# A fused attention, Fourier, MLP and rotation kernel: a layernorm's small values put in PSUM, and single columns and a row of the transform handled in another way

## The chip, the cores and the metric

The kernel runs on one core of one Trainium2 chip. The metric is the device time of one execution in microseconds (us), lower is better; the shown time of a kernel is the median of its runs.

## The reference

Three blocks follow each other. Attention on 2 batches, 8 heads, 768 positions of 64 values, where a query sees only the keys of its own hash bucket (the signs of six projections). Then the real part of a two-dimensional Fourier transform is added, and a layernorm feeds a two-layer MLP. Then an angle per element turns the values into two parts, which are mixed over the positions, and a last layer is added.

```
mask = q_bucket[:, :, :, None] == k_bucket[:, :, None, :]
attn = softmax(where(mask, q @ k^T / 8, -1e9)) ; x = attn @ v        # (2, 768, 512)

mixed = real(fft(fft(x, axis=1), axis=2))
u  = x + mixed
un = (u - mean(u)) / sqrt(var(u) + 1e-6)                               # over the 512 columns
x  = u + relu(un @ w_ch1) @ w_ch2                                      # 512 -> 2048 -> 512

theta = x @ w_theta
y = w_tok_r @ (x * cos(theta)) + w_tok_i @ (x * sin(theta))            # over the 768 rows
u = x + y
out = u + relu(u @ w_ch)
```

## The kernel before

**Number format.** Large matrices are split into a high and a low part (16-bit or a rounded 32-bit format) and multiplied in three passes (high by high, high by low, low by high). That is why many names come as pairs: `w1h`, `w1l`; `hh`, `hl`; `wthh`, `wthl`. The high part is made by ScalarE (ACT), the low part by VectorE (DVE) or GpSimd (POOL), which subtracts the high part from the original.

**Stages.** A batch has six row tiles of 128 x 512. Attention goes by tiles of 128 queries of one head, 48 tiles a batch: scores on TensorE (PE, matmuls `pss<-stk`, four of 128x384 a tile), the row maximum on DVE (`nm`), the exponential on ACT (`p`), its masking on POOL (`p<-p,p`, `pt`), a transposing DMA (`pt<-p`), and the product with the values on PE (`pso<-vv,pt`). The transform (`Fft`) folds the rows on DVE as the heads come in (`fold`, `part`), then `rest` multiplies with the cosine and sine tables on PE (first `ps<-h,ct`, then `psm<-dt,fa`, whose last matmuls of a tile read `hlz`) and adds the result to `u` on DVE. `rest` yields after each of its three column groups, each with two of the six row tiles.

**The layernorm** (`ln_scale`, line 706) works on two row tiles at a time: BN_STATS and BN_AGGR give mean and variance `mv`, and then twelve DVE instructions on 128x2 values compute the inverse square root `rs`: `ve` is the variance plus 1e-6, an integer shift (`t<-ve`) and an integer multiply-add (`rs<-t`) give a first guess, and three Newton steps of three instructions refine it (`t<-rs,ve`, `t<-t,rs`, `rs<-t,rs`). All of it is in SBUF. `ln_first` does this for the first two row tiles of batch zero: DVE makes `un`, PE transposes it (`psm<-ident,un`). The other five pairs go through `layernorm`: ACT and DVE make the two halves of `u2`, and a transposing DMA on the SP queue writes them to `unT`.

**The MLP.** `mlp1` multiplies `unT` with `w1` in tiles of two 128-column groups (`psm<-unT,w1h` and `psm<-unT,w1l`, 24 matmuls of 256 columns), `mlp2` multiplies the result with `w2` (matmuls of 512 columns, called `w2` matmuls below; 96 a group).

**What sets the order.** A framework schedules each engine's instructions from priorities: `at(us)` sets the due time of what is written next, and a model of the machine orders the instructions of each engine. So the MLP of batch zero, the attention of batch one and the transform of batch one are interleaved: the scheduler decides how many MLP matmuls stand between two score tiles, and a change of a few instructions can change that order. PSUM has eight banks, taken in rings: while attention runs, three of one bank each (`psm`, taken by `PS1()` in turn for the transform, the layernorm's transposes and the MLP), two double ones for scores (`pss`) and one for the attention output (`pso`); after it, five more single ones (`psf`).

**Lines the change touches.** `Fft.__init__` (544) makes the fold buffer `fa`; `part` makes the difference or sum of mirrored columns, `one` (574) handles the one column that has no mirror partner; `fold` (580) calls them. In `rest` (612) the transform's last step keeps two lone columns per row tile in exchanged places and swaps them through `lone`, and copies row 0 of tile 3 to `row` before a single-row sum is added. Constants come from `_constants`; its table `so` holds the sines of odd frequencies.

Of the kernel before, what the change touches and what calls it, by code (L numbers as in the profile page):

```python
# [33 lines left out]
def f(t):  # L34
    return t.bitcast(F32)
# [35 lines left out]
def fused_kernel(ctx, tc, A, out):  # L71
# [469 lines left out]
    class Fft:  # L541


        def __init__(self, b, side):
            self.b, self.p = b, pool(f"ft{b}", 1, side=side)
            ft = self.p
            self.fa = mk(ft, [128, 4608], F32, "fa")
            self.fm = self.fa[:, 0:3072].rearrange("p (a n) -> p a n", a=6)
            self.y1 = self.fa[:, 3072:4608].rearrange("p (a n) -> p a n", a=6)
# [23 lines left out]

        def one(self, nm, i, a):

            hl = self.hl[nm][:, :, :, i:i + 1]
            V.tensor_copy(out=hl[:, 0], in_=a)
            V.tensor_tensor(out=hl[:, 1], in0=a, in1=f(hl[:, 0]), op=ALU.subtract)

        def fold(self, p):  # L580
# [20 lines left out]
            if p in (1, 2) and 3 - p in self.done:  # L601
                self.part("e", slice(65, 128), ALU.subtract, y1[:, 0:self.ne, 65:128], y1[:, 0:self.ne, 191:128:-1])
                yield
                self.part("o", slice(64, 127), ALU.add, y1[:, 3:6, 65:128], y1[:, 3:6, 191:128:-1])
                self.one("o", 127, y1[:, 3:6, 128:129])
                yield
            if len(self.done) == 4:
                self.part("e", slice(1, 65), ALU.subtract, y1[:, 0:self.ne, 1:65], y1[:, 0:self.ne, 255:191:-1])
                self.one("e", 0, y1[:, 0:self.ne, 0:1])
                self.part("o", slice(0, 64), ALU.add, y1[:, 3:6, 1:65], y1[:, 3:6, 255:191:-1])  # L610

        def rest(self):
# [3 lines left out]
            if self.ne == 4:  # L616
                er = hl["e"][0:1, :, 3]
            else:

                er = hl["o"][0:1, :, 0]  # L620
                er0 = mk(ft, [1, 128], F32, "zraw", bufs=2 - self.b)
                V.tensor_tensor(out=er0[:, 1:128], in0=y1[0:1, 3, 1:128], in1=y1[0:1, 3, 255:128:-1], op=ALU.subtract)
                V.tensor_copy(out=er0[:, 0:1], in_=y1[0:1, 3, 0:1])
                V.tensor_copy(out=er[:, 0], in_=er0)
                V.tensor_tensor(out=er[:, 1], in0=er0, in1=f(er[:, 0]), op=ALU.subtract)
# [8 lines left out]
            for tt in (0, 3):  # L634
                for c in (0, 256):
                    cc = 192 + (c if tt == 0 else 256 - c)
                    pl_copy(u[:, tt:tt + 3, cc:cc + 1], x[:, tt:tt + 3, c:c + 1])
            alt2 = alt.unsqueeze(1).to_broadcast([1, 193, 2])
            acs = mk(ft, [128, 4608], F32R, "fa")
# [35 lines left out]
            for t in range(3):  # L675
# [11 lines left out]
                if t == 0:  # L687
                    row = mk(ft, [1, DM], F32, "hle")
                    V.tensor_copy(out=row, in_=u[0:1, 3])
# [8 lines left out]
                V.tensor_copy(out=mid, in_=u[:, 3 + t, 448:191:-256])  # L698
                V.tensor_copy(out=u[:, 3 + t, 192:449:256], in_=mid)
# [7 lines left out]
    def ln_scale(b, g, p):  # L707
# [3 lines left out]
        v, r, t = (mk(p, [128, n], F32, f"{k}{g[0]}") for k in ("ve", "rs", "t2"))  # L711
        for i in range(n):
# [4 lines left out]
        V.tensor_scalar(out=t.bitcast(I32), in0=v.bitcast(I32), scalar1=1, scalar2=None, op0=ALU.logical_shift_right)  # L717
        V.tensor_scalar(out=r.bitcast(I32), in0=t.bitcast(I32), scalar1=-1.0, scalar2=1597463007.0,
                        op0=ALU.mult, op1=ALU.add)
# [4 lines left out]
        return mv, r, t  # L724

    def ln_first():

        mv, rs, _ = ln_scale(0, (0, 2), so_p)
# [13 lines left out]
    def layernorm(b, m_p, ln_p, res, groups):  # L742
        u = u_t[b]
        unT = res[b] = mk(m_p, [128, 8, S], F16, "unT")
        for g in groups:
            mv, rs, t2 = ln_scale(b, g, ln_p)
# [326 lines left out]
def _constants():  # L1073
# [15 lines left out]
    s2, so, s0 = cs(np.sin, d, k2), cs(np.sin, d + 1, ko), cs(np.sin, d, k0)  # L1089
    dt = np.concatenate([cs(np.cos, d, k) for k in (k2, ko, k0, ku)] + [  # L1090
# [59 lines left out]
```

## Time and profile before

| | |
|---|---|
| median of three runs | 759.32 us (758.41 to 765.56) |
| profiled execution, device time | 759.25 us |
| its span in the trace | 757.5 us |
| PE busy | 672.4 us, 89% |
| DVE busy | 440.9 us, 58% |
| ACT busy | 400.3 us, 53% |
| POOL busy | 370.7 us, 49% |
| chain that ended last | PE 43%, DVE 15%, issue 12%, ACT 11%, POOL 10%, DMA 9% |

How to read it: busy times are those of one profiled execution, which the trace covers from its first to its last instruction (the span); device time has 1.75 us more around it. The chain that ended last is followed back from the last instruction, at each step to what released it, so its shares name the engines that were waited for. In rows of the trace, `out<-in` are the program's buffer names, shapes are partitions x elements, `xcount` folds equal neighbours on one engine, and `[5.67 <-DVE un L62]` is idle time ahead of an instruction with what ended it. PEclk is the clock that TensorE was granted, as a share of 2.4 GHz.

### The profile page before, as it was taken

The page shows a single profiled execution, that of the slowest core. Times are in us where ns is not written, and L with a number is a line of the kernel's source. Part 1 is how long each engine was busy: PE and PEld are TensorE (multiplying, and loading weights), DVE is VectorE, ACT ScalarE, POOL GpSimd, SP SyncE. Part 2 cuts the span into 40 slices and gives each one's busy share as a digit, 9 for nine tenths or more (in the row PEclk, how much of TensorE's full clock was granted, in tenths as well). Part 3 has the DMA queues.
Part 4 walks back from the last instruction along what each step waited for, and adds up shares of the span by engine and source line. Part 5 has one row for each costly group of instructions (what it writes and reads, how often), then busy time and mean ns, then how long its engine had stood idle before and what let it go on. Part 6 is the DMA issues. An engine that isn't in the chain of part 4 may idle for free.

```text
span 757.5 us, 13333 instructions
## 1 busy us (share of the span) xinstructions
PE 672.4 (89%) x5300; PEld 526.5 (70%) x5300; DVE 440.9 (58%) x710; ACT 400.3 (53%) x639; POOL 370.7 (49%) x302
## 2 busy tenths in 40 slices
PE   6979775859397997999989979999999989999997
PEld 2767564647286555786676757587485778998997
DVE  6778879698889855543386782055332266552122
ACT  4787595967588798763322151064325555662010
POOL 4786778697666779776560110033403235841000
PEclk8999997969689998999999989999999999999999
DMA  9685768479687999878650061011003611362202
GB/s 321 150 171 102 167 126 167 94 207 195 184 183 166 228 239 262 158 141 120 114 184 7 5 157 29 1 42 29 1 1 126 201 29 43 110 217 77 84 1 83
DMA packets 151358, 93.19 MB, mean 123 GB/s; under 512 B 126272, under 2 KB 136704, under 8 KB 151296
## 3 DMA queue, kind: packets, MB, share of 16 engines
q1 hardware_dynamic: 149424, 85.87, 48.3%
q0 software_dynamic: 1872, 6.47, 2.4%
q8 instruction: 41, 0.67, 0.4%
q14 instruction: 21, 0.17, 0.1%
HBM read 49.62 MB, written 6.29 MB: 74 GB/s over the span
## 4 chain that ended last, share of the span: by engine, by line
PE 43%; DVE 15%; issue 12%; ACT 11%; POOL 10%; DMA 9%; POOLq 0%; SPq 0%; ACTq 0%; DVEq 0%
PE psm L62 26%; PE psf L62 10%; DMA r<-in_wtok 3%; ACT r L62 3%; DMA pt<-p 2%; POOL p L62 2%; PE pss L64 2%; DVE fa L64 2%; DVE nm L64 2%; POOL w1l L62 2%; ACT stk L64 2%; DVE r L62 2%; PE psm L64 2%; DVE fa L62 1%; DMA r<-in_w 1%
## 5 line engine op out<-in xcount | busy, mean ns | idle before, releaser
L62 PE MATMUL psm<-unT,w1h 128*128 128x256 f16 x768 | 131.9, 276 | 7.9 <-DMA unT<-u 4.5
L62 PE MATMUL psm<-unT,w1l 128*128 128x256 f16 x384 | 105.9, 276 | 0.0
L62 PEld LDWEIGHTS <-w1h 128*128 128x128 f16 (+1 forms) x774 | 75.6, 99 | 24.3 <-issue 11.6
L62 DVE SCALAR_TENSOR_TENSOR r<-r 128x512 uint32<-128x512 uint32 (+1 forms) x64 | 59.0, 923 | 55.3 <-ACT r L62 49.5
L64 PE MATMUL pss<-stk 128*128 128x384 f32 x192 | 51.4, 390 | 26.6 <-ACT p L64 6.7
L62 POOL TENSOR_TENSOR w1l<-r,w1h 128x384 fp32r<-128x384 f32 (+1 forms) x36 | 41.0, 1148 | 58.4 <-ACT w1h L62 58.2
L62 PEld LDWEIGHTS <-hh 128*128 128x128 f16 x384 | 37.2, 99 | 43.1 <-issue 2.7
L62 DVE TENSOR_REDUCE nm<-pss 128x1 f32<-128x768 f32 x48 | 45.1, 950 | 34.9 <-PE pss L62 34.9
L62 ACT ACTIVATE r<-r,chalf 128x512 uint32<-128x512 uint32 (+1 forms) x64 | 46.2, 722 | 33.1 <-DMA r<-in_wtok 17.0
L62 POOL TENSOR_TENSOR p<-p,p 128x768 f16<-128x768 f32 x32 | 55.3, 1731 | 15.9 <-ACT p L62 14.3
L62 DVE SCALAR_TENSOR_TENSOR hl<-psm,hh 128x512 f16<-128x512 f32 x48 | 32.9, 686 | 48.9 <-ACT hh L62 48.8
L62 PE MATMUL psm<-w2l,hh 128*128 128x512 f16 x192 | 61.2, 385 | 0.0
L62 PE MATMUL psm<-w2h,hl 128*128 128x512 f16 x192 | 61.0, 383 | 0.0
L62 PE MATMUL psm<-w2h,hh 128*128 128x512 f16 x192 | 60.5, 382 | 0.0
L62 ACT ACTIVATE hh<-psm 128x512 f16<-128x512 f32 x48 | 28.4, 592 | 57.6 <-PE psm L62 57.5
L62 ACT ACTIVATE p<-pss,nm 128x768 f32<-128x768 f32 x48 | 42.7, 894 | 27.9 <-DVE nm L62 26.4
L62 PE MATMUL pss<-stk 128*128 128x384 f32 x192 | 50.7, 389 | 7.6 <-ACT p L62 6.4
L64 PEld LDWEIGHTS pss<-stk 128*128 128x128 f32 x192 | 34.4, 207 | 31.1 <-ACT p L64 8.2
L64 DVE TENSOR_REDUCE nm<-pss 128x1 f32<-128x768 f32 x48 | 45.5, 950 | 15.7 <-PE pss L64 15.4
L62 PEld LDWEIGHTS pss<-stk 128*128 128x128 f32 x192 | 35.1, 206 | 12.0 <-ACT p L62 8.9
L62 POOL TENSOR_SCALAR nn<-nn 128x512 f32<-128x512 f32 x12 | 7.9, 655 | 71.1 <-ACT nn L62 71.1
L62 PEld LDWEIGHTS <-w1l 128*128 128x128 f16 x384 | 38.0, 99 | 6.5 <-issue 1.8
(297 smaller groups left out, 1682.9 us busy)
## 6 DMA issues: line engine op xcount, KB each, us to landing
r<-in_w SPq DMA_DIRECT2D x32, 512.0 KB, 4.6
r<-in_wtok SPq DMA_DIRECT2D x24, 384.0 KB, 3.8
stk<-stk SPq DMA_DIRECT2D x28, 192.0 KB, 3.3
vr<-in_v SPq DMA_DIRECT2D x8, 390.0 KB, 4.6
tt<-in_qT SPq DMA_DIRECT2D x8, 384.0 KB, 3.6
tt<-in_kT SPq DMA_DIRECT2D x8, 384.0 KB, 4.4
xT<-xs SPq DMA_DIRECT2D x12, 256.0 KB, 2.6
xt<-xT SPq DMA_DIRECT2D x4, 768.0 KB, 5.6
```

The source lines that it names most:

```text
L62: return fn(*a, **k)
L64: self.last = fn(*a, **k)
```

## The change

*Layernorm.* `ln_scale` takes a PSUM tile `few` from `PS1()` and keeps `ve` and `t` in it; `rs` and `mv` stay in SBUF. The shift is gone: one integer multiply-add by -0.5 makes the first guess, so the chain has 11 instructions. `layernorm` makes its own small `t2` in SBUF for the product of mean and deviation.

*Lone columns.* The fold buffer has a column more in each of six parts, set to zero once, so that the column without a partner meets a zero or, where the sine table's column 127 is halved, itself. `one` and its instructions are gone; `part` works on slices one column wider. In the single-row sum two DVE copies are gone and one is made by ACT.

*Row copy and swaps.* Row 0 of tile 3 is copied by POOL, ahead of the transform's multiplications, to a place that is free by then. The swaps of the lone columns, six pairs of 128x2 copies, are made by ACT in place of DVE.

```diff
-            self.fa = mk(ft, [128, 4608], F32, "fa")
+            self.fa = mk(ft, [128, 4614], F32, "fa")
-            self.y1 = self.fa[:, 3072:4608].rearrange("p (a n) -> p a n", a=6)
+            self.y1 = self.fa[:, 3072:4614].rearrange("p (a n) -> p a n", a=6)
+            V.memset(self.y1[:, :, 256:257], 0.0)
...
-        def one(self, nm, i, a):
-
-            hl = self.hl[nm][:, :, :, i:i + 1]
-            V.tensor_copy(out=hl[:, 0], in_=a)
-            V.tensor_tensor(out=hl[:, 1], in0=a, in1=f(hl[:, 0]), op=ALU.subtract)
...
-                self.part("o", slice(64, 127), ALU.add, y1[:, 3:6, 65:128], y1[:, 3:6, 191:128:-1])
-                self.one("o", 127, y1[:, 3:6, 128:129])
+                self.part("o", slice(64, 128), ALU.add, y1[:, 3:6, 65:129], y1[:, 3:6, 191:127:-1])
...
-                self.part("e", slice(1, 65), ALU.subtract, y1[:, 0:self.ne, 1:65], y1[:, 0:self.ne, 255:191:-1])
-                self.one("e", 0, y1[:, 0:self.ne, 0:1])
+                self.part("e", slice(0, 65), ALU.subtract, y1[:, 0:self.ne, 0:65], y1[:, 0:self.ne, 256:191:-1])
...
-                V.tensor_tensor(out=er0[:, 1:128], in0=y1[0:1, 3, 1:128], in1=y1[0:1, 3, 255:128:-1], op=ALU.subtract)
-                V.tensor_copy(out=er0[:, 0:1], in_=y1[0:1, 3, 0:1])
-                V.tensor_copy(out=er[:, 0], in_=er0)
+                V.tensor_tensor(out=er0, in0=y1[0:1, 3, 0:128], in1=y1[0:1, 3, 256:128:-1], op=ALU.subtract)
+                AC.activation(out=er[:, 0], in_=er0, func=AF.Copy)
...
+            row = x[0:1, 5] if self.b else un0[0:1, 1]
+            pl_copy(row, u[0:1, 3])
...
-                if t == 0:
-                    row = mk(ft, [1, DM], F32, "hle")
-                    V.tensor_copy(out=row, in_=u[0:1, 3])
...
-                V.tensor_copy(out=mid, in_=u[:, 3 + t, 448:191:-256])
-                V.tensor_copy(out=u[:, 3 + t, 192:449:256], in_=mid)
+                AC.activation(out=mid, in_=u[:, 3 + t, 448:191:-256], func=AF.Copy)
+                AC.activation(out=u[:, 3 + t, 192:449:256], in_=mid, func=AF.Copy)
...
-        v, r, t = (mk(p, [128, n], F32, f"{k}{g[0]}") for k in ("ve", "rs", "t2"))
+        r = mk(p, [128, n], F32, f"rs{g[0]}")
+        few = PS1()
+        v, t = few[:, 0:n], few[:, 8:8 + n]
...
-        V.tensor_scalar(out=t.bitcast(I32), in0=v.bitcast(I32), scalar1=1, scalar2=None, op0=ALU.logical_shift_right)
-        V.tensor_scalar(out=r.bitcast(I32), in0=t.bitcast(I32), scalar1=-1.0, scalar2=1597463007.0,
-                        op0=ALU.mult, op1=ALU.add)
+        V.tensor_scalar(out=r.bitcast(I32), in0=v.bitcast(I32), scalar1=-0.5, scalar2=1597463007.0, op0=ALU.mult, op1=ALU.add)
...
+            t2 = mk(ln_p, [128, g[1] - g[0]], F32, f"t2{g[0]}")
...
+    so[127] *= 0.5
```

**Where instructions move.** PE has as many instructions as before, and so has the SP queue; DVE has 28 fewer (684 in place of 712), ACT 13 more, POOL 2 more. PE's order is unchanged up to the first transform matmul of batch zero and again from batch one's MLP on; between them it differs. At the 16th, 24th, 32nd and 48th score tile of batch one, the MLP of batch zero has done 73, 200, 266 and 384 of its 576 first-layer matmuls before, and 0, 170, 208 and 384 after; of its 288 `w2` matmuls 0, 50, 96 and 185 before, and 0, 0, 96 and 132 after. The pieces below show the places that matter. First DVE, from the second BN_AGGR of the first layernorm to `un`; numbers behind names are buffer numbers. Before:

```order
L62 BN_AGGR mv_2278<-bs 128x2
L62 TENSOR_SCALAR ve_2279<-mv_2278 128x2
L62 TENSOR_SCALAR t_2281<-ve_2279 128x2
L62 TENSOR_SCALAR rs_2280<-t_2281 128x2
L62 TENSOR_REDUCE nm<-pss 128x1
L62 TENSOR_TENSOR t_2281<-rs_2280,ve_2279 128x2
L62 SCALAR_TENSOR_TENSOR r_2123<-r_2123 128x512
L62 SCALAR_TENSOR_TENSOR t_2281<-t_2281,rs_2280 128x2
```

The same place after the change, up to the first Newton step:

```order
L62 BN_AGGR mv_2274<-bs 128x2
L62 SCALAR_TENSOR_TENSOR r_2106<-r_2106 128x512
L62 TENSOR_TENSOR x<-pso,r 128x6x64
L62 TENSOR_SCALAR psm<-mv_2274 128x2
L62 TENSOR_REDUCE nm<-pss 128x1
L62 TENSOR_SCALAR rs_2275<-psm 128x2
L62 SCALAR_TENSOR_TENSOR r_2113<-r_2113 128x512
L62 TENSOR_TENSOR psm<-rs_2275,psm 128x2
```

A weight conversion (`r`) and a scaling of attention output (`x`) have come in behind BN_AGGR; before `un` there are in all three conversions, two reductions `nm` and one scaling, where there were one conversion and one reduction. Next PE, at the transposes of the first layernorm (`un_110`), which stood apart around one score tile. Before:

```order
L62 MATMUL pso<-vv,pt 128x65
L62 MATMUL psm<-ident,un_110 128x128 x4
L62 MATMUL pss<-stk 128x384 x4
L62 MATMUL psm<-ident,un_110 128x128 x4
L62 MATMUL psm<-dt,fa 128x2x64 x6
```

After:

```order
L62 MATMUL psm<-ident,un_110 128x128 x8
L62 MATMUL psm<-dt,fa 128x2x64 x6
L62 MATMUL psm<-dt,fa 128x2x128 x6
L62 MATMUL psm<-dt,fa 128x2x64 x3
L62 MATMUL psm<-dt,hlz_2236 128x2x64 x3
L62 MATMUL pss<-stk 128x384 x4
```

The eight transposes now follow each other, all behind the twelfth score tile of batch one, where the first four stood behind the eleventh. Last ACT at the end of batch one's transform, where the swaps stand. Before:

```order
L62 ACTIVATE fa<-psf 128x386
L62 ACTIVATE hlz_5279<-psf 128x384
L62 ACTIVATE wthh<-r_5479 128x512
L62 ACTIVATE wthh<-r_5486 128x512
L62 ACTIVATE wthh<-r_5493 128x512
```

After:

```order
L62 ACTIVATE fa<-psf 128x386
L62 ACTIVATE hlz_5268<-psf 128x384
L62 ACTIVATE lone<-u_5107 128x2
L62 ACTIVATE u_5107<-lone 128x2
L62 ACTIVATE lone<-u_5107 128x2
L62 ACTIVATE u_5107<-lone 128x2
L62 ACTIVATE lone<-u_5107 128x2
L62 ACTIVATE u_5107<-lone 128x2
L62 ACTIVATE wthh<-r_5463 128x512
L62 ACTIVATE wthh<-r_5470 128x512
```

The three pairs of swaps stand ahead of the `wthh` conversions, which make the high part of `w_theta`. In batch zero the swaps stand among exponentials (`p<-pss,nm`) and weight conversions (`w1h<-r`), some of which come between the two copies of a pair. On PE, between the last transform matmul of batch one and the first of batch one's MLP that reads batch one's `unT`, there stood 56 `w2` matmuls and one set of transposes; now 82 `w2` matmuls stand ahead of it.

## Rows read from the trace of the kernel before

**Rows 1.** Stages: us; PE, PEld, DVE, ACT, POOL busy (instructions); PEclk, DMA, GB/s.

```profile
197.00:209.20 12.20, 2.91 (x23) 2.15 (x22) 11.82 (x16) 4.52 (x7) 10.40 (x8) 0.50 0.81 212
209.20:427.10 217.90, 203.46 (x1887) 152.16 (x1887) 135.56 (x219) 129.75 (x190) 133.88 (x101) 0.97 0.73 156
427.10:444.30 17.20, 12.72 (x62) 5.93 (x61) 17.17 (x69) 7.96 (x15) 4.70 (x4) 0.95 0.41 107
444.30:449.60 5.30, 5.25 (x26) 3.83 (x27) 3.62 (x7) 1.43 (x4) 0.42 (x1) 0.52 0.77 151
```

**Rows 2.** Timeline of PE: start, length, instruction, [idle before].

```profile
199.40 1.65 PE L62 MATMUL pss<-stk 128*128 128x384 f32 x4 [2.31 <-ACT p L62]
...
209.22 1.11 PE L62 MATMUL psm<-ident,un 128*128 128x128 f32 x4 [5.67 <-DVE un L62]
```

**Rows 3.** Groups of DVE, 197 to 207.2 us: count, busy us, mean ns.

```profile
L62 DVE SCALAR_TENSOR_TENSOR t<-t,rs 128x2 f32<-128x2 f32 x3 | 1.9, 623 | 0.1
L62 DVE TENSOR_SCALAR t<-ve 128x2 int32<-128x2 int32 x1 | 1.6, 1569 | 0.0
L62 DVE TENSOR_TENSOR t<-rs,ve 128x2 f32<-128x2 f32 x3 | 1.5, 507 | 0.1
L62 DVE TENSOR_SCALAR ve<-mv 128x2 f32<-128x2 f32 x1 | 1.4, 1411 | 0.0
L62 DVE TENSOR_SCALAR rs<-t 128x2 int32<-128x2 int32 x1 | 1.1, 1076 | 0.0
L62 DVE SCALAR_TENSOR_TENSOR rs<-t,rs 128x2 f32<-128x2 f32 x3 | 1.1, 358 | 0.1
L62 DVE TENSOR_REDUCE nm<-pss 128x1 f32<-128x768 f32 x1 | 0.9, 945 | 0.0
L62 DVE SCALAR_TENSOR_TENSOR r<-r 128x512 uint32<-128x512 uint32 x1 | 0.7, 678 | 0.0
```

**Rows 4.** Timeline of DVE at the second layernorm's first chains.

```profile
432.94 1.17 DVE L62 SCALAR_TENSOR_TENSOR t<-t,rs 128x2 f32<-128x2 f32 x1
...
434.11 1.27 DVE L62 TENSOR_SCALAR ve<-mv 128x2 f32<-128x2 f32 x1
...
435.37 1.26 DVE L62 TENSOR_TENSOR t<-rs,ve 128x2 f32<-128x2 f32 x1
...
436.62 0.15 DVE L62 TENSOR_TENSOR t<-rs,ve 128x2 f32<-128x2 f32 x1
```

**Rows 5.** Timeline of POOL beside the two chains.

```profile
196.33 3.68 POOL L62 TENSOR_TENSOR p<-p,p 128x768 f16<-128x768 f32 x2
...
432.77 3.83 POOL L62 TENSOR_TENSOR wthl<-r,wthh 128x512 fp32r<-128x512 f32 x3 [37.59 <-ACT wthh L62]
```

**Rows 6.** Timeline of PE ahead of batch one's MLP.

```profile
438.79 0.59 PE L62 MATMUL psm<-w2h,hl 128*128 128x512 f16 x2
439.22 0.60 PE L62 MATMUL psf<-ident,u 128*128 128x128 f32 x4
444.35 0.59 PE L62 MATMUL psm<-unT,w1h 128*128 128x256 f16 x2 [4.53 <-DMA unT<-u]
```

**Rows 7.** Groups of the whole span: DVE twice, ACT, POOL.

```profile
L62 DVE TENSOR_TENSOR hle<-fa,hle 128x4 fp32r<-128x4 f32 x1 | 2.6, 2554 | 0.0
...
L62 DVE TENSOR_SCALAR r<-pso 128x6 f32<-128x6 f32 x8 | 1.2, 155 | 5.0 <-PE pso L62 5.0
...
L62 ACT ACTIVATE hle<-zraw 128x189 fp32r<-128x189 f32 x1 | 0.4, 360 | 3.1 <-DVE hlo L62 3.1
...
L62 POOL TENSOR_SCALAR u<-x 128x384 f32<-128x384 f32 x4 | 4.1, 1028 | 5.9 <-PE pso L62 5.9
```

**Rows 8.** Timeline of ACT ahead of the second layernorm.

```profile
432.01 1.80 ACT L62 ACTIVATE wthh<-r 128x512 fp32r<-128x512 f32 x3 [10.95 <-DVE mv L62]
```

**Rows 9.** Timeline of DVE: the last value of batch zero's third chain.

```profile
239.42 0.14 DVE L62 SCALAR_TENSOR_TENSOR rs<-t,rs 128x2 f32<-128x2 f32 x1
```

**Rows 10.** Timeline of PE: third MLP tile's start, batch zero.

```profile
226.00 0.38 PE L62 MATMUL psm<-unT,w1h 128*128 128x256 f16 x2
```

More of the change, by code (lines that the diff above doesn't have):

```diff
@@ L637, in rest @@
                     pl_copy(u[:, tt:tt + 3, cc:cc + 1], x[:, tt:tt + 3, c:c + 1])
+            row = x[0:1, 5] if self.b else un0[0:1, 1]
+            pl_copy(row, u[0:1, 3])
             alt2 = alt.unsqueeze(1).to_broadcast([1, 193, 2])
-            acs = mk(ft, [128, 4608], F32R, "fa")
+            acs = mk(ft, [128, 4614], F32R, "fa")
             off = [0]
@@ L723, in ln_scale @@
             V.scalar_tensor_tensor(out=r, in0=t, scalar=1.5, in1=r, op0=ALU.add, op1=ALU.mult)
-        return mv, r, t
+        return mv, r
     def ln_first():
-        mv, rs, _ = ln_scale(0, (0, 2), so_p)
+        mv, rs = ln_scale(0, (0, 2), so_p)
         for i in range(2):
@@ L745, in layernorm @@
         for g in groups:
-            mv, rs, t2 = ln_scale(b, g, ln_p)
+            mv, rs = ln_scale(b, g, ln_p)
+            t2 = mk(ln_p, [128, g[1] - g[0]], F32, f"t2{g[0]}")
             gate[b] = V.scalar_tensor_tensor(out=t2, in0=mv[:, :, 0], scalar=-1.0, in1=rs, op0=ALU.mult, op1=ALU.mult)
```

## The prediction, made before the changed kernel ran

> **What bounds the kernel now.** I read the table of stages first [rows 1]: each row gives the busy time of the engines in a stretch. TensorE (PE) fills most of the span: from 209.2 us to 427.1 it is busy 203.5 of 217.9. In two short stretches it stands. From 197.0 to 209.2 it works 2.9 of 12.2 us while VectorE (DVE) works 11.8; from 427.1 to 444.3 it works 12.7 of 17.2 while DVE works all of it. In both, a layernorm's inverse deviation is computed. So the question is what the change does to these two waits, and whether the time stays won.
>
> The first wait is in PE's timeline [rows 2]: the transposes of `un` start at 209.22 after 5.67 us of idling for DVE. What DVE did is in the grouped rows [rows 3]: 12 instructions on 128x2 values, the chain `ve`, `t`, `rs`, take 8.6 us (1.9 + 1.6 + 1.5 + 1.4 + 1.1 + 1.1). One such instruction takes 0.15 us where nothing holds it (the last line of [rows 4]); the long ones run beside GpSimd (POOL) instructions, such as 3.68 us of `p` [rows 5]. The second layernorm shows it more sharply: three chain instructions last 1.17, 1.27 and 1.26 us [rows 4] while POOL's three `wthl` subtractions run, 3.83 us from 432.77 [rows 5]; the next take 0.15 again. So a DVE instruction of this chain can be held until a POOL instruction ends.
>
> The Trainium skill says this in "SBUF — State Buffer", section "Who interferes with whom": a DVE instruction with two SBUF inputs, or in a two-port mode, contends with a GpSimd instruction that reads SBUF, and one with a single SBUF input outside those modes does not. The trace agrees for the held side (1.17 against 0.15 us); no row of before has these instructions with an operand in PSUM.
>
> The second wait is 4.53 us for the transposed `unT` [rows 6]. Behind it PE runs at half clock: 444.3 to 449.6 has a granted clock of 0.52, nearly all at the lower level of 1.2 GHz [rows 1].
>
> **The change, part by part.**
>
> *Chain values in PSUM.* With no hold left, the first chain falls from 8.6 us to 11 instructions of 0.15, that is 1.7: 6.9 us won. With full hold nothing is won. I take the end near no hold: the held rows read only SBUF, often twice, and no new instruction of the chain has two SBUF inputs (`t` and `v` are in PSUM, `r` and `mv` in SBUF). For the price of a PSUM operand the nearest row reads PSUM on 128x6 in 155 ns [rows 7], no more than SBUF; a write of small values to PSUM is in no row, so I bound it by nothing and by another 0.15 us an instruction, 1.7 us a chain, and take nothing. `un` and the weight conversions keep SBUF operands and can still be held.
>
> The Trainium skill has a rule against the change: "Perfetto Trace Analysis", section "Optimizing Scalar/DVE Operations", puts DVE's access overhead at about 60 ns on SBUF and 125 on PSUM. By it 11 instructions would cost 0.7 us more (an estimate from that page), inside the bound above; the row with a PSUM source shows no such difference.
>
> *Order around the first chain.* DVE's order now has two conversions `r`, one reduction `nm` and one scaling `x` more between the second aggregate and `un`. At 0.68 and 0.95 us [rows 3], the scaling taken as a conversion, they take back 3.0 of the 6.9 us, though that work is not owed later. PE's wait of 5.67 us shrinks by 3.9 to 5.67; I take 4.5.
>
> *Order around the second chain.* The three holds lie 3.3 us above 3 x 0.15 [rows 4]. More follows from PE's order: between the last transform matmul and the first that needs `unT` stood 56 `w2` matmuls and one set of transposes; now 82 `w2` matmuls stand there. At two every 0.43 us [rows 6] they are 17.6 us of work. `unT` came 17.2 us after the last transform matmul (427.1 to 444.3), and should now come after some 13.9. Either is under 17.6, so the wait of 4.53 goes even if the chain wins nothing. With it goes the half clock: 5.3 us at 0.52 lose 2.5. Together 7.0.
>
> *What covers it must come from somewhere.* PE's instructions are the same in number. When the second batch's last scores are issued, 132 of the MLP's `w2` matmuls stand ahead of them instead of 185: 53 fewer, 11.5 us at 0.216. That work comes later, so PE has less to fill its earlier gaps with. From 209.2 to 427.1 it idles 14.4 us already [rows 1]. If the softmax of the second batch moves up as far as PE's work is taken out, nothing is lost; if not, 11.5 us are. The engines of the softmax were busy 62% (DVE, 135.6 of 217.9) and 61% (POOL), PE 93%, so PE mostly set the pace: I take 2.5.
>
> *Swaps on ScalarE (ACT).* Six pairs, at most 0.36 us an instruction by the nearest row, of 189 columns [rows 7]. ACT waits there for DVE's add. Behind it queue, in batch zero, an exponential or weight conversion, which the score tiles wait for; in batch one, three `wthh` conversions, which already stood idle 10.95 us for this place [rows 8]. DVE adds other tiles meanwhile; only the last pair before a chain is uncovered, 0.7 us, and in batch one the `w2` work covers that. Uncovered, all would cost 12 x 0.36 = 4.3.
>
> *Lone columns and row copy.* Of the removed DVE instructions one was dear because it was held: 2.55 us for the four-column subtraction [rows 7]. A neighbour with two SBUF inputs inherits such a hold, so I count 0.5 of a possible 2.5, swaps included. POOL's copies of one row cost about what its copies of 384 columns do, 1.03 us [rows 7], off the path: the copy is needed a whole group of matmuls later. The ACT copy in the single-row sum is hidden the same way, the two memsets (nearest row 128x6, 0.155 us [rows 7]) stand where DVE is not waited for, the parts are a column wider, and the halved constant is made on the host: nothing.
>
> *The rest.* PE's order is the same row by row up to the first transform matmul of batch zero at 160.8 us, and from batch one's MLP at 444.3 to the end. A difference must arise between.
>
> The sum: 4.5 + 7.0 + 0.5 - 2.5 = 9.5 us off 759.25, the profiled execution's own time (span 757.5 plus 1.75 around it; the median of the runs is 759.32). That is 749.8.
>
> **The rivals.**
>
> *First gain absorbed.* Behind 209 us PE, DMA, POOL and ACT take turns, so the 4.5 us may be waited for elsewhere, and the small gain too. What is left is 7.0 - 2.5: 754.8. It also holds if the chain stays held in PSUM, so that the change doesn't do what it says, since the cover of the second wait does not depend on it. For it speaks that PE waited 2.31 us for an ACT-made operand in the same stretch [rows 2].
>
> *Filler missed.* The second batch's softmax does not move up, and PE idles the whole 11.5 us: 759.25 - 4.5 - 7.0 + 11.5 = 759.2. Against it speaks PE's 93%.
>
> *Slower: the bank that holds the chain.* The chain's values now keep one of three `psm` banks until `rs` is done. The MLP's tiles of batch zero come behind the second and third chain in that ring. Before, the third chain's last `rs` was written at 239.42, while the third tile's matmuls began at 226.00 [rows 9, 10]. If the chains run no faster and this order stays, PE stands from 226.0 to 239.6, 13.6 us, and runs cold for another 2.5 behind it. With the first and small gains gone: 759.25 - 7.0 + 13.6 + 2.5 = 768.4. It decides from a wait of about 14 us in all. Against it: in the new order the MLP begins four softmax tiles later, after most of these chains.
>
> **How the numbers follow.** Forecast 0.53, absorbed 0.20, filler missed 0.15, bank 0.12. About 1% (7.6 us) is what a measurement of this kernel tells from no change. Faster, under 751.7, is the forecast's share, 0.53; slower, over 766.9, the bank's, less a little, 0.11; the rest 0.36. The range runs from 743 (waits of 5.67 and 7.0 gone, 4 from the small parts' bounds, nothing given back, gives 742.6) to 762 (filler missed with a first gain of only 1.7); that leaves out the bank's case and a tail of the others. The forecast's own range is 743 to 752.
>
> **What would show it.** Chain instructions of about 0.15 us beside busy POOL show the PSUM step right; of 1 us, wrong. No wait for `un` over 1.5 us shows the first gain. PE without a gap before batch one's MLP, and a clock of 1.0 there, shows the second; if that MLP then begins later than some 437 us, the filler was missed. A PE wait for `rs` at batch zero's second or third MLP tile shows the bank. The forecast is wrong if PE's idle time between 209 and 427 grows by over 5 us.

## The result, and the profile after

The changed kernel takes 754.34 us, the median of eight runs (750.65 to 756.07), against 759.96 us before, taken on the same chip. The ratio is 0.9911 with a 95% interval of [0.9883, 0.9939]: 5.6 us less. A second set of six runs gave 754.42 us and 0.9912 [0.9882, 0.9941]. The execution that was profiled first is the fastest of the fourteen, 750.65 us with a span of 748.6; the second profiled one took 753.04 us with a span of 751.2.

The table of stages, cut at the same matmuls in both kernels: from the first transform matmul of batch zero to the transposes of `un`, from there to the last score matmul of batch one, and to the last transform matmul of batch one. What stands between two cuts is not quite the same, since PE's order differs: in the changed kernel one score tile more with its products stands in the first stage, and in the second that tile and 53 `w2` matmuls are missing. Columns as in [rows 1]. Before:

```profile
160.82:209.22 48.40, 33.84 (x229) 26.67 (x229) 43.82 (x57) 32.49 (x52) 35.07 (x25) 0.71 0.75 184
209.22:372.66 163.44, 151.39 (x1472) 110.14 (x1473) 100.76 (x152) 117.76 (x167) 119.49 (x82) 0.95 0.88 181
372.66:427.29 54.63, 52.26 (x418) 42.16 (x416) 34.96 (x67) 11.99 (x23) 14.38 (x19) 1.00 0.29 80
```

After, with two stages more, from the last transform matmul to the first matmul of batch one's MLP, and the 5.3 us behind that:

```profile
160.55:203.26 42.71, 35.14 (x272) 28.03 (x272) 34.06 (x55) 35.11 (x58) 34.75 (x25) 0.78 0.79 186
203.26:362.87 159.61, 139.85 (x1381) 104.73 (x1379) 98.82 (x144) 116.16 (x168) 121.03 (x84) 0.95 0.92 192
362.87:419.38 56.51, 55.32 (x433) 43.02 (x431) 34.30 (x61) 12.10 (x26) 14.66 (x21) 1.00 0.29 77
419.38:436.92 17.54, 17.54 (x82) 7.92 (x81) 15.33 (x63) 9.74 (x19) 5.10 (x4) 1.00 0.51 123
436.92:442.22 5.30, 5.30 (x38) 3.64 (x37) 2.05 (x4) 2.98 (x5) 0.00 (x0) 1.00 1.03 188
```

The last two rows answer to the last two of [rows 1]: PE now works through, at a clock of 1.00 where 0.95 and 0.52 stood. The stage ahead of batch one's MLP is no shorter for it, 17.5 us against 17.1 (427.29 to 444.35): the wait is filled with `w2` matmuls from earlier stages. The first row is 5.7 us shorter. The second is shorter by 3.8 us, but PE is idle in it for 19.8 us (159.61 less 139.85), where it was idle for 12.1.

PE's timeline of the changed kernel, which answers to [rows 2] and [rows 6]:

```profile
203.26 1.09 PE L62 MATMUL psm<-ident,un 128*128 128x128 f32 x4
204.76 1.09 PE L62 MATMUL psm<-ident,un 128*128 128x128 f32 x4 [0.41 <-DVE un L62]
...
224.27 1.65 PE L62 MATMUL pss<-stk 128*128 128x384 f32 x4 [4.96 <-ACT p L62]
```

The wait of 5.67 us for `un` is down to 0.41 ahead of the second set of transposes. A wait of 4.96 us has come 20 us later, for the exponential of a score tile.

The layernorm's chain in DVE's timeline, which answers to [rows 3] and [rows 4]; first a part of the first chain, then rows of the second layernorm's chains, the last of them `t` from `mv` and `rs`, which the change left in SBUF:

```profile
199.00 0.15 DVE L62 TENSOR_TENSOR psm<-rs,psm 128x2 f32<-128x2 f32 x1
199.19 0.17 DVE L62 SCALAR_TENSOR_TENSOR psm<-psm,rs 128x2 f32<-128x2 f32 x1
199.39 0.16 DVE L62 SCALAR_TENSOR_TENSOR rs<-psm,rs 128x2 f32<-128x2 f32 x1
```

```profile
423.44 0.14 DVE L62 TENSOR_SCALAR rs<-psf 128x2 int32<-128x2 int32 x1
...
423.71 0.16 DVE L62 TENSOR_SCALAR psf<-mv 128x2 f32<-128x2 f32 x1
...
425.93 0.16 DVE L62 SCALAR_TENSOR_TENSOR psf<-psf,rs 128x2 f32<-128x2 f32 x1
426.00 0.69 DVE L62 SCALAR_TENSOR_TENSOR t<-mv,rs 128x2 f32<-128x2 f32 x1
```

And what POOL did beside them, which answers to [rows 5]:

```profile
198.48 1.62 POOL L62 TENSOR_TENSOR w1l<-r,w1h 128x512 f16<-128x512 f32 x1
...
200.88 1.58 POOL L62 TENSOR_TENSOR w1l<-r,w1h 128x512 f16<-128x512 f32 x1
```

```profile
422.87 3.81 POOL L62 TENSOR_TENSOR wthl<-r,wthh 128x512 fp32r<-128x512 f32 x3 [27.73 <-ACT wthh L62]
```

The chain's instructions take 0.15 to 0.17 us beside a POOL that is busy from 198.48 on. At 426.00 POOL's 3.81 us of `wthl` still run, to 426.68: the instruction that reads two operands from SBUF lasts 0.69 us and ends with them; its neighbour with one operand in PSUM took 0.16 us. Instructions with a single input belong here too. In the kernel before, three of them that went from SBUF to SBUF, `ve<-mv`, `t<-ve` and `rs<-t`, were as long as the held ones, 1.41, 1.57 and 1.08 us [rows 3]; with PSUM at one end the two that are left take 0.16 and 0.14 us beside `wthl` (423.71 and 423.44).

### The profile page after: what moved, and what is told of

Read it like the earlier page. It is cut to its first block, busy times and chain, and to the rows that moved or that the text cites. A ratio compares the mean times of both kernels' runs of the same rounds, so it can differ in the third digit from the quotient of the medians.

```text
span 748.6 us, 13328 instructions
## 1 busy us (share of the span) xinstructions
PE 670.2 (90%) x5300; PEld 525.8 (70%) x5300; DVE 424.8 (57%) x682; ACT 402.8 (54%) x652; POOL 373.1 (50%) x304
## 4 chain that ended last, share of the span: by engine, by line
PE 46%; issue 12%; ACT 11%; DVE 11%; DMA 10%; POOL 9%; SPq 0%; POOLq 0%; DVEq 0%; ACTq 0%
PE psm L62 29%; PE psf L62 10%; DMA r<-in_wtok 4%; ACT r L62 2%; DVE fa L64 2%; POOL p L62 2%; POOL w1l L62 2%; PE pss L64 2%; DVE nm L64 2%; PE pss L62 2%; DMA pt<-p 2%; DMA r<-in_wth 2%; ACT stk L64 1%; ACT p L62 1%; PE psm L64 1%
## 5 line engine op out<-in xcount | busy, mean ns | idle before, releaser
L62 DVE SCALAR_TENSOR_TENSOR r<-r 128x512 uint32<-128x512 uint32 (+1 forms) x64 | 54.2, 847 | 73.0 <-ACT r L62 64.5
L62 PE MATMUL psm<-w2l,hh 128*128 128x512 f16 x192 | 59.4, 382 | 0.0
L62 PEld LDWEIGHTS pss<-stk 128*128 128x128 f32 x192 | 34.8, 206 | 19.5 <-ACT p L62 14.7
```

The lines of the kernel that those rows point to most:

```text
L62: return fn(*a, **k)
```

## The experiments

All times are medians, and ratios are taken to runs of the kernel before on the same chip, with 95% intervals. The idle times of PE below are those of one profiled execution, whose time stands beside the median: the length of a stage less PE's busy time in it, worked out from tables of stages like the ones above. Idle time between the last scores and the last transform matmul, 2.4 us before and 1.2 in the change, is in no column. Two limits go with the columns. The change and e1 are the same kernel and differ by 2.0 us in each of the first two, so that a smaller difference says nothing. And where the profiled execution lies far from the median (3 to 4 us in the change, e3, e9 and e12), they explain the median only in part.

| kernel | us | profiled | ratio to before | idle to `un` | idle `un` to last scores | idle ahead of batch one's MLP | idle behind |
|---|---|---|---|---|---|---|---|
| before | 759.96 | 759.25 | | 14.6 | 12.1 | 4.5 | 10.1 |
| the change | 754.34 | 750.65 | 0.9911 [0.9883, 0.9939] | 7.6 | 19.8 | 0.0 | 9.7 |
| e1, the change again | 754.42 | 753.04 | 0.9912 [0.9882, 0.9941] | 5.6 | 17.7 | 0.0 | 10.5 |
| e2, `t` in SBUF | 761.55 | 763.07 | 1.0006 [0.9981, 1.0031] | 12.5 | 20.3 | 0.0 | 13.0 |
| e3, all in SBUF | 764.07 | 767.17 | 1.0036 [1.0014, 1.0058] | 12.8 | 21.8 | 0.0 | 14.7 |
| e4, PSUM part alone | 756.92 | 755.55 | 0.9946 [0.9928, 0.9965] | 8.4 | 21.4 | 0.0 | 13.2 |
| e5, swaps on DVE | 754.74 | 755.12 | 0.9913 [0.9885, 0.9941] | 8.4 | 19.6 | 0.0 | 12.3 |
| e6, lone columns as before | 759.06 | 759.82 | 0.9985 [0.9960, 1.0009] | 9.1 | 22.8 | 0.0 | 11.2 |
| e7, row copy as before | 750.20 | 749.16 | 0.9860 [0.9835, 0.9886] | 8.9 | 14.5 | 0.0 | 10.2 |
| e8, MLP due 10 us sooner | 752.60 | 752.52 | 0.9897 [0.9873, 0.9921] | 5.6 | 20.0 | 0.1 | 10.6 |
| e9, PSUM and lone columns | 755.98 | 752.93 | 0.9932 [0.9905, 0.9958] | 9.1 | 15.8 | 0.0 | 9.5 |
| e10, e7 and e8 together | 749.41 | 748.77 | 0.9854 [0.9826, 0.9882] | 9.2 | 16.5 | 0.2 | 12.6 |
| e11, lone columns alone | 755.24 | 756.11 | 0.9948 [0.9921, 0.9976] | 11.8 | 15.4 | 0.0 | 15.9 |
| e12, e7 and MLP due 20 us sooner | 759.05 | 754.98 | 0.9968 [0.9939, 0.9997] | 9.1 | 14.4 | 6.5 | 10.8 |

**e1: the change again.** No edit.

> The changed kernel again, to see how its executions spread: the profiled one took 750.65 us, the median of eight was 754.34. If the spread comes from one place, a second profile that is 2 us or more longer shows the extra time in one stretch; I expect that stretch between the first transform matmul of batch zero and the last score tile (160 to 350 us), where DMA transfers, softmax and MLP share the engines, and not behind batch one's MLP, whose order and clock are steady. Expected median 754, ratio 0.990 to 0.993.

The median came as expected, the place of the spread did not. To the last scores the second profiled execution is 0.3 us later than the first (363.17 against 362.87), and the MLP of batch one starts 0.3 us later; 2.3 us of the 2.6 between the two spans arise behind it. The rows show where. PE waits for the high part of token weights in both; the rows are first those of the faster, then of the slower execution, each wait with a stretch of 5 us behind it as in the table of stages:

```profile
675.21 0.44 PE L62 MATMUL psm<-w1h,zb 128*128 128x384 f32 x1 [1.82 <-ACT w1h L62]
```

```profile
676.92:681.92 5.00, 5.00 (x30) 4.89 (x30) 0.59 (x2) 0.75 (x2) 1.92 (x2) 1.00 0.48 157
```

```profile
676.36 0.44 PE L62 MATMUL psm<-w1h,zb 128*128 128x384 f32 x1 [2.11 <-ACT w1h L62]
```

```profile
677.24:682.24 5.00, 5.00 (x22) 5.00 (x21) 0.58 (x2) 1.06 (x3) 2.18 (x3) 0.66 0.53 161
```

The wait is 0.3 us longer, and the clock behind it is 0.66 in place of 1.00, so some 3.4 of the 5 us ran at 1.2 GHz. From this matmul to the end of the span the slower execution takes 74.8 us, the faster 73.4: 1.4 of the 2.3 us. Ahead of the wait, ACT's conversions had waited for the DMA of the weights, 2.12 and 1.05 us in the faster execution, 2.19 and 1.14 in the slower. So a part of the spread of this kernel is made long after the change, where a DMA has its share in how long PE waits, and the clock adds to it.

**e2: one value back in SBUF.**

```diff
-        r = mk(p, [128, n], F32, f"rs{g[0]}")
+        r, t = (mk(p, [128, n], F32, f"{k}{g[0]}") for k in ("rs", "t2"))
         few = PS1()
-        v, t = few[:, 0:n], few[:, 8:8 + n]
+        v = few[:, 0:n]
```

> The change with one value of the chain, t, back in SBUF (in the place of t2); the variance plus 1e-6 stays in PSUM. TensorE's order is that of the change. Two of the three instructions of a Newton step then read two SBUF operands. My theory (operands in PSUM end the hold): these instructions take 0.3 to 1.2 us beside POOL again, the wait for un comes back with 2 to 5 us, and the time is 755 to 758 us, 1 to 4 us over the change; the wait ahead of batch one's MLP stays away, since 82 w2 matmuls still cover it. Rival (only the new order counts): time as the change, within 1 us.

761.55 us: all of the gain is gone, with TensorE's order that of the change and POOL's too (on ACT and on DVE two instructions each stand a few places away, at 233 to 240 us). The place is the one named, the size is over the range. DVE's timeline in the first chain, then POOL's and PE's:

```profile
198.71 0.14 DVE L62 TENSOR_TENSOR t<-rs,psm 128x2 f32<-128x2 f32 x1
198.89 0.95 DVE L62 SCALAR_TENSOR_TENSOR t<-t,rs 128x2 f32<-128x2 f32 x1
199.87 0.75 DVE L62 SCALAR_TENSOR_TENSOR rs<-t,rs 128x2 f32<-128x2 f32 x1
200.66 0.16 DVE L62 TENSOR_TENSOR t<-rs,psm 128x2 f32<-128x2 f32 x1
...
203.38 0.16 DVE L62 TENSOR_TENSOR t<-rs,psm 128x2 f32<-128x2 f32 x1
203.57 1.65 DVE L62 SCALAR_TENSOR_TENSOR t<-t,rs 128x2 f32<-128x2 f32 x1
...
205.75 1.76 DVE L62 SCALAR_TENSOR_TENSOR rs<-t,rs 128x2 f32<-128x2 f32 x1
```

```profile
203.41 4.08 POOL L62 TENSOR_TENSOR stk<-tt,stk 64x768 fp32r<-64x768 f32 x2
```

```profile
209.06 1.11 PE L62 MATMUL psm<-ident,un 128*128 128x128 f32 x4 [5.90 <-DVE un L62]
```

Three kinds of instruction alternate on the same 128x2 values. `t<-rs,psm`, with one operand in PSUM, takes 0.14 to 0.16 us each time; `t<-t,rs` and `rs<-t,rs`, with both in SBUF, take 0.75 to 1.76 us in this chain. The wait for `un` is 5.90 us, as in [rows 2] (5.67). This is the cleanest of the experiments, since little but the place of one operand differs. It agrees with what the Trainium skill says in "SBUF — State Buffer", section "Who interferes with whom", of two SBUF inputs against one. The wait ahead of batch one's MLP stays away, as expected, but the second chain is held again (its first `t<-t,rs` takes 1.05 us, `rs<-t,rs` 1.17), and at 450.69 PE waits 1.09 us for DVE's `u`. The part behind the MLP's start is 316.4 us long, against 311.7 and 314.0 in the two profiles of the change; most of that is not traced to the hold.

**e3: all small values in SBUF, 11 instructions.**

```diff
-        r = mk(p, [128, n], F32, f"rs{g[0]}")
-        few = PS1()
-        v, t = few[:, 0:n], few[:, 8:8 + n]
+        v, r, t = (mk(p, [128, n], F32, f"{k}{g[0]}") for k in ("ve", "rs", "t2"))
```

> The change with all small values back in SBUF, still 11 instructions, no PSUM bank taken. TensorE's order differs a little from the change's, but 82 w2 matmuls still stand ahead of batch one's MLP. My theory: chain held again, wait for un 4 to 6 us, no wait ahead of batch one's MLP as long as unT comes within 17.7 us of the last transform matmul; time 756 to 759. Rival (order alone makes the gain): 753 to 755. Rival (the held second chain makes unT late in spite of the cover): a wait of 1 to 4 us there and 759 to 761.

764.07 us, slower than before by its interval, and above every range given. The wait for `un` is 6.07 us, about as expected, and there is no wait ahead of batch one's MLP. So in this order the cover alone wins nothing: idle time to the last scores is 21.8 us, no less than in the change (19.8 and 17.7), and behind the MLP's start PE is idle for 14.7 us where it was 10.1 before. In both e2 and e3 the first wait is as long as before, and yet PE idles 8 to 10 us more up to the last scores than the kernel before: that idle time is not the first gain waited for elsewhere. The instruction that was saved is worth nothing that shows here.

**e4: the layernorm's part alone.** The kernel before, with `ln_scale` and its callers as in the change.

> The kernel before with the layernorm's part of the change alone (values in PSUM, 11 instructions); lone columns, row copy and swaps as before. 71 w2 matmuls, 15.3 us, stand ahead of batch one's MLP, and unT should come some 14 us after the last transform matmul. My theory (PSUM values and the order that comes with them carry the change): both waits gone, 752 to 756 us. Rival (the small edits carry it): 757 to 760.

756.92 us, 3.7 us less than the runs beside it (760.64), just above my range and below the rival's. Both waits are gone, as expected. It keeps less than the change: on the same chip e1 has 754.42, and five of its six executions lie below all twelve of e4, though the intervals of the two ratios overlap.

**e5, e6, e7: the change with one of its small parts undone.**

```diff
# e5
-                AC.activation(out=mid, in_=u[:, 3 + t, 448:191:-256], func=AF.Copy)
-                AC.activation(out=u[:, 3 + t, 192:449:256], in_=mid, func=AF.Copy)
+                V.tensor_copy(out=mid, in_=u[:, 3 + t, 448:191:-256])
+                V.tensor_copy(out=u[:, 3 + t, 192:449:256], in_=mid)
# e6
-                self.part("o", slice(64, 128), ALU.add, y1[:, 3:6, 65:129], y1[:, 3:6, 191:127:-1])
+                self.part("o", slice(64, 127), ALU.add, y1[:, 3:6, 65:128], y1[:, 3:6, 191:128:-1])
+                self.one("o", 127, y1[:, 3:6, 128:129])
...
# e7
-            row = x[0:1, 5] if self.b else un0[0:1, 1]
-            pl_copy(row, u[0:1, 3])
...
+                    row = mk(ft, [1, DM], F32, "hle")
+                    V.tensor_copy(out=row, in_=u[0:1, 3])
```

> The change without the move of the swaps: the six pairs of 128x2 copies stay on VectorE (about 0.15 us each), all else as in the change. TensorE's order is near that of the change, with 149 in place of 132 w2 matmuls ahead of batch one's last scores and 82 covering unT. My theory (the PSUM chain and the cover carry the gain, the swaps nothing): 753 to 757 us. Rival (the swaps on ScalarE delay exponentials and with them the scores of batch one): 749 to 752, and less than 5 us of TensorE waiting for p between the first layernorm and the last scores, where the change waited 7.5. Rival (the swaps on ScalarE are worth something): 757 to 760.

> The change without the lone columns' part: separate one-column instructions, no zero column, no halved constant; PSUM values, row copy and swaps as in the change. TensorE's order is 0.82 like the change's. My theory: the held four-column subtraction comes back on VectorE, at most 2.5 us, ahead of the first transform; 754 to 758 us. Rival (this part carries a good share of the gain): over 759.

> The change without POOL's copy of one row: VectorE copies it as before (1.07 us on average). My theory: nothing that can be measured, 753 to 757 us. Rival (the copy on VectorE delays the layernorm's first aggregate): 757 to 760, and a wait for un of over 1.5 us.

e5 came as expected: no worth of the swaps is seen either way (754.74). e6 took 759.06 us, above my range and just inside the rival's (over 759): 2.5 us more stand ahead of the first transform (163.1 us against 160.6), and 3.1 us more idle time in batch one's attention. e7 fits neither line of its expectation: it is faster than the change, 750.20 us, though the wait for `un` is 2.12 us; the two intervals just touch. The gain lies in batch one's attention, where PE is idle for 14.5 us in place of 19.8 (17.7 in e1).

What made the wait of 4.96 us that e7 does not have can be read from ACT's queue. The changed kernel at that place, ACT and then DVE:

```profile
220.83 0.67 ACT L62 ACTIVATE w1h<-r 128x512 f16<-128x512 f32 x1 [1.54 <-DVE r L62]
221.40 0.84 ACT L62 ACTIVATE vv<-vr 128x780 f16<-128x780 f32 x1
222.14 0.75 ACT L62 ACTIVATE r<-r,chalf 128x512 uint32<-128x512 uint32 x1
222.79 0.66 ACT L62 ACTIVATE r<-r 128x512 f32<-128x512 f32 x1
223.34 0.88 ACT L62 ACTIVATE p<-pss,nm 128x768 f32<-128x768 f32 x1
```

```profile
217.20 1.98 DVE L62 TENSOR_REDUCE nm<-pss 128x1 f32<-128x768 f32 x2
219.10 1.70 DVE L62 SCALAR_TENSOR_TENSOR r<-r 128x512 uint32<-128x512 uint32 x1
```

The same place in e7, ACT:

```profile
219.23 0.77 ACT L62 ACTIVATE r<-r,chalf 128x512 uint32<-128x512 uint32 x1
219.89 0.66 ACT L62 ACTIVATE r<-r 128x512 f32<-128x512 f32 x1
220.45 0.88 ACT L62 ACTIVATE p<-pss,nm 128x768 f32<-128x768 f32 x1
```

In the change the row maxima `nm` of two tiles are ready by 219.18 (217.20 and 1.98). The first exponential that needs one starts at 223.34, because four other instructions stand ahead of it in ACT's queue: a weight conversion, which waits 1.54 us for DVE's `r` (1.70 us long beside POOL; 0.68 in [rows 3]), then `vv` and two steps of the next conversion. In e7 two conversion steps precede the exponential at that place, and PE waits 0.70 us for it. The row copy itself cannot cost this: POOL's copies take 0.9 us. That the order of the queue makes the difference is what these rows suggest; the order was not changed by itself. Nor is it this place alone: at 239.16 e7 waits 4.24 us for DVE's `bits`, where the change waits 2.23.

**e8: the MLP due 10 us sooner.**

```diff
-        w2=100.0, w2s=1.0, m0=170.0, ...
+        w2=100.0, w2s=1.0, m0=160.0, ...
```

> The change with the MLP of batch zero due 10 us sooner (its due time 160 in place of 170), which moves nothing up to the 40th score tile of batch one and then puts 48 more w2 matmuls (10.4 us) ahead of batch one's last scores; 61 w2 matmuls and one set of transposes (14.1 us) are left to cover unT. If the lost filler cost the time at the end of batch one's attention, the idle time of TensorE between the first layernorm and the last scores falls by over 3 us and the time to 750 to 752. My theory (the idle time lies in the first 12 tiles behind the layernorm, 205 to 260 us, where the MLP has not begun or unT has only just come): the idle time and the time stay, 753 to 756; unT is covered just so, with a wait under 1 us.

752.60 us, between the rival's range and mine. Idle time to the last scores stayed, 20.0 against 19.8 us, as I expected, and no wait for `unT` shows: the `w2` matmuls that were put back there filled none of it. The time is lower by 1.7 us, but its interval overlaps the change's, so this is not told from no difference.

**e9: PSUM values and lone columns without the two moves.** Row copy and swaps as before.

> The kernel before with the PSUM values and the lone columns' part alone; row copy and swaps stay on VectorE. If the edits' worths simply add (the change at 754.4; without the row copy's move 750.2; without the swaps' move 754.7), this is at 750 to 751. My theory is that none of the two moves costs or wins by itself, and that each reshuffles the order of softmax and MLP in batch one's attention: then 750 to 756, with the idle time of TensorE between the first layernorm and the last scores (19.8 us in the change, 14.5 without the row copy's move) telling where in that range.

755.98 us. If the worths of the parts added, it would be at 750. They don't: the median, in the upper end of the wider range, is not told from the change's. The low idle time to the last scores, 15.8 us, is that of an execution 3 us below the median.

**e10 and e12: the row copy as before, with the MLP due 10 and 20 us sooner** (`m0=160.0` and `m0=150.0`).

> The change with the row copied by VectorE as before, and the MLP of batch zero due 10 us sooner (160 in place of 170): 180 in place of 132 w2 matmuls ahead of batch one's last scores. If the two gains, 4.2 us and 1.8 us, add: 748 to 749 us. If the second is not a gain of its own: 750.

> As the last but one, with the MLP due 20 us sooner (150): its first-layer matmuls now also fill the tiles right behind the layernorms (165 in place of 88 at the 20th score tile of batch one), and 31 w2 matmuls with parts of the next stage cover unT. If filler behind the layernorms is what TensorE lacks there, its idle time between the first layernorm and the last scores falls by over 3 us, 746 to 749. Against it stands that unT of batch zero must then be there sooner: if it is not, TensorE waits for it and the time is 750 to 756.

e10 gave the lowest time of all, 749.41 us and 0.9854 [0.9826, 0.9882]; its interval ends where the change's begins, and it is not told apart from e7 alone (0.9860). e12 lost nearly all of it, 759.05 us, above both of its ranges. Its idle time to the last scores is that of e7, 14.4 us, so more filler behind the layernorms fills nothing there; what it took from the cover is paid ahead of batch one's MLP, where parts of the next stage had been put in the place of `w2` matmuls and wait for their operands. The execution shown is 4.1 us faster than the median, so this is not the whole loss. PE's timeline of e12:

```profile
433.75 0.50 PE L62 MATMUL psf<-wthh,xh 128*128 128x512 f32 x1 [1.18 <-ACT xh L62]
...
440.39 0.80 PE L62 MATMUL psf<-wthh,xh 128*128 128x512 f32 x1 [3.73 <-ACT wthh L62]
...
444.01 0.61 PE L62 MATMUL psm<-unT,w1h 128*128 128x256 f16 x2 [1.01 <-DMA unT<-u]
```

**e11: the lone columns' part alone.**

> The kernel before with the lone columns' part alone: no PSUM values. 82 w2 matmuls stand ahead of batch one's MLP, as in the change. My theory: the chain is held as before, the wait for un is 4 to 6 us, no wait ahead of batch one's MLP; cover without the PSUM values did not show as a gain in the run with all values in SBUF (764.1), so 757 to 763. Rival (the lone columns carry a share of their own, as the 4.7 us lost without them suggest): 753 to 757.

755.24 us, in the rival's range and not mine, without a value in PSUM. It is not told from e9, 755.98 on the same chip, which has the PSUM values besides: in this order they are worth nothing that shows. The wait for `un` is 2.30 us. DVE's and POOL's timelines show why:

```profile
198.77 1.57 DVE L62 TENSOR_SCALAR t<-ve 128x2 int32<-128x2 int32 x1
200.38 1.07 DVE L62 TENSOR_SCALAR rs<-t 128x2 int32<-128x2 int32 x1
...
202.46 0.16 DVE L62 SCALAR_TENSOR_TENSOR rs<-t,rs 128x2 f32<-128x2 f32 x1
```

```profile
201.39 0.83 POOL L62 TENSOR_SCALAR p<-p 128x768 f16<-128x768 f32 x1
205.68 1.81 POOL L62 TENSOR_TENSOR stk<-tt,stk 64x768 fp32r<-64x768 f32 x1 [3.46 <-issue]
```

In this kernel's order POOL has nothing to do from 202.2 to 205.7 us, and the chain's later instructions fall into that pause and take 0.15 or 0.16 us. So the hold needs both, operands in SBUF and a busy POOL beside them, and an order that leaves a pause does part of what PSUM does. There is no wait ahead of the MLP, but 8 us into it, where ACT's half of `u` stands behind a conversion that waits 3.93 us for the DMA of token weights:

```profile
443.12 0.38 PE L62 MATMUL psm<-unT,w1h 128*128 128x256 f16 x2 [4.11 <-DVE u L62]
```

## Why the prediction was right, and where it was not

The time lies in the stated range, 743 to 762 us, but outside the forecast's own, 743 to 752. Both waits went as forecast; more was given back between them.

**The hold, and the price of PSUM.** Right. The chain's instructions take 0.15 to 0.17 us beside a busy POOL, and e2 shows that with a second operand in SBUF they are held. Reads and writes of PSUM cost nothing that shows, so of the two bounds (nothing, or 0.15 us an instruction) the lower was the right end.

**The first wait.** Right in kind, small in size. I took 4.5 of 5.67 us; the wait shrank by 5.3, and PE's idle time up to the transposes by 7.0 (14.6 to 7.6; by 9.0 in e1), in part because one score tile more stands there.

**The second wait and the clock behind it.** Right: 4.53 us gone, and a clock of 1.00 in the 5.3 us behind. The reason was too simple. I wrote that the wait goes even if the chain wins nothing; e2 and e3 bear that out for this one wait, but not as a gain: PE idles longer ahead of it, and 13.0 and 14.7 us behind it where it was 10.1. (Idle time behind is no sign of a held chain by itself: e4, whose chain is free, has 13.2.) In the change, too, the wait was paid for elsewhere: from the transposes of `un` to batch one's MLP PE was idle for 19.0 us before, this wait included, and is for 21.0 now (19.0 in e1).

**What was given back.** This is the step that failed: I took 2.5 us, and said that the forecast is wrong if PE's idle time between 209 and 427 us grows by over 5. From the transposes of `un` to the last transform matmul it grew from 14.4 us by 6.5 in the first profiled execution, over that limit, and by 4.5 in e1, under it; either is well over 2.5. I had argued from the engines' busy shares that PE sets the pace there. The shares are means over 218 us, and the waits lie at a few places where one queue runs its instructions in an order that does not fit, such as the exponential that came 4.2 us after its operand. The rival that I called absorbed, to which I gave 0.20, has its number, 754.8 us, where the median came out, but that is luck. In it the first gain is waited for elsewhere; in e2 and e3, which lack the first gain, PE idles as long up to the last scores. Missed filler doesn't describe it either: batch one's MLP began at 436.92 us, at the limit of 437 that I had set, and yet with `w2` matmuls put back (e8) the idle time stayed. What fits the runs is the order of batch one's attention.

**The small parts.** Their prices were within the bounds: swaps 0.20 us an instruction (bound 0.36), POOL's copies 0.9 and 0.8 (1.03), memsets 0.06. The groups of the changed kernel:

```profile
L62 ACT ACTIVATE u<-lone 128x2 f32<-128x2 f32 x6 | 1.2, 202 | 0.1
```

```profile
L62 POOL TENSOR_SCALAR un<-u 1x512 f32<-1x512 f32 x1 | 0.9, 908 | 0.0
L62 POOL TENSOR_SCALAR x<-u 1x512 f32<-1x512 f32 x1 | 0.8, 786 | 8.6 <-DVE fa L62 8.6
```

```profile
L62 DVE MEMSET fa<- 128x6 f32 x2 | 0.1, 63 | 0.0
```

But what a part costs by itself is not what it is worth here: taking out the row copy's move wins 4.1 us, and taking out the lone columns loses 4.7, each with another order of batch one's attention.

**The slow rival.** It did not come. No wait for `rs` at batch zero's MLP is left, the one of 1.36 us before included: in the new order that MLP starts at 226.74 us in place of 218.70.

**The sum.** In the first pair of profiled executions, 757.5 and 748.6 us of span, idle time fell by 6.8 us and busy time by 2.1: 8.9 us, near the 9.5 that I summed. That is luck twice. The terms erred both ways, the first wait by 2.5 us too little and what was given back by 4.0 too little; and the execution is the fastest of the change, while the one that I started from stood near its median. By medians 5.6 us remain. The rows show where the two part. PE's order is the same again from the second tile of batch one's MLP on (not from the first, as I wrote: 12 `w2` matmuls and a set of transposes have moved behind that one). The second tile starts at 449.38 us before, at 442.86 in the change and at 443.17 in e1, 6.5 and 6.2 us sooner with the same PE work done. The rest of the 8.9 arises behind it, at one place above all; before, then after:

```profile
608.73 0.50 PE L62 MATMUL psf<-wthh,xh 128*128 128x512 f32 x1 [2.06 <-ACT xh L62]
```

```profile
601.20 0.50 PE L62 MATMUL psf<-wthh,xh 128*128 128x512 f32 x1 [1.15 <-ACT xh L62]
```

In the 5 us behind these two the clock is 0.66 before and 1.00 after. e1 has 1.18 us and 1.00 there and loses as much again at the token weights. So some 6.2 to 6.5 us go with the change's order and PSUM values, and the sum had no term for what single executions win or lose behind batch one's MLP.

**What stays open.** It is open why the part behind the MLP's start is 316 to 320 us long in e2, e3 and e11; 4.1 us of it in e11 is the wait for `u` shown above, and e7, whose chain is free, has 315.4. Open too is which of the many moved instructions makes the idle time of batch one's attention 14.5 or 19.8 us. The runs show that it goes with the order, not which instruction decides it.

## What to carry to other kernels

Small values that a vector engine reads and writes many times beside a busy GpSimd belong in PSUM, or one of their two operands does: here that is 7.1 us between two kernels that differ in little else (the change and e2). It is not a fixed price: the same values in PSUM were worth 3.7 us in e4, and nothing that shows between e11 and e9, where e11's order leaves GpSimd a pause beside the first chain. What a shortened layernorm chain wins can be paid back in the queues behind it, so look at the place where the freed engine meets its next operand, not at the mean busy share. And where a scheduler decides the order, the worths of single edits don't add: time each combination.

## What the runs showed of the hardware that was not expected

Writing and reading small values in PSUM was not dearer for VectorE than SBUF: 0.14 to 0.17 us with one operand there, 0.14 to 0.16 us without one where nothing held it. A 128x2 instruction with a single input from SBUF was held as those with two were, 1.08 to 1.57 us in the kernel before. And the clock behind a wait of PE differed between two executions of one kernel, 1.00 after 1.82 us of waiting and 0.66 after 2.11; with it went 1.4 us of the 2.3 that arose behind the start of batch one's MLP.
